# Fewer plain fp32 steps in block 0, zero matmuls in the prologue, new planner durations and other staging tiles in a pooled-attention and two-MLP kernel

## The chip, the cores and the metric

The kernel runs on one NeuronCore of one Trainium2 chip. The metric is the time of one execution in microseconds of the device (us), the median of several. Engine names are those of the profile: PE (matrix engine), DVE (vector engine), ACT (scalar engine), POOL, SP (here a queue that issues DMAs).

## What is computed

The reference pools keys and values over groups of 8 rows, does softmax attention for 8 batches of 8 heads, and passes the 4608 rows of 512 through two MLPs:

```python
k_p = k.reshape(B, H, Sp, pool, D).mean(axis=3)        # pool = 8, S = 576, D = 64
v_p = v.reshape(B, H, Sp, pool, D).mean(axis=3)
attn = softmax(scale * q @ k_p.T) ; x = attn @ v_p      # rows of all heads: 4608 x 512
h = x @ w_in                                            # 512 x 2048
g = where(h >= 1, h, where(h <= -1, 0, (h + 1)**2 / 4))
x = g @ w_out                                           # 2048 x 512
out = (sigmoid(x @ w_gate) * (x @ w_val)) @ w_out2      # 512 x 1536, twice, and 1536 x 512
```

The weights come in as float64 and are rounded on the chip.

## The kernel before, in words

**Blocks and steps.** The 4608 rows are nine blocks of 512. The first MLP runs blocks 0 to 6 one after the other (the rest goes through a form with seven products in place of eight, later in the program). A block has 16 steps, one for each 128 columns of `w_in`. A step m makes `hps` = 128 columns of x @ w_in (function `columns`), the activation g from it (L741 and L743 on ACT, L746 on DVE), and adds g times 128 rows of `w_out` to four accumulators (the out GEMM, L765 to L775).

**Three products or one.** A matmul of fp32 precision is made of three in a faster type (`three`, L609 to L611): each operand is split in a high part (a cast on ACT, L534) and a low part (a subtraction on DVE, L543). In the out GEMM of block 0 the first `PLAIN` = 12 steps skip this: they multiply the unsplit fp32 tiles (L772), so that neither g nor the `w_out` tile (`wj`) has to be split.

**Weights.** During block 0 all 16 tiles of `w_in` (`win`) and of `w_out` (`wout_f`) are loaded as float64 bit patterns and converted (function `weight`): two passes on ACT (L580, L582), four on DVE (L585, L587, L590, L594), and for `win` the split (L534, L543).

**Prologue.** Ahead of block 0 stand four units, one for each pair of heads: `pooled` sums the keys on DVE (L339) and turns them on PE (L360), sums the values either on PE (`add_values`, L375, eight matmuls with the identity) or, for the pairs in `DVE_VALUES` = (2, 3), on DVE (L339), and `unit` turns q (L407), makes scores (L436), softmax (L445 to L455, ACT L448), turns the weights (L470), multiplies by the values (L508) and splits the result into an x tile (L515, L522). Attention for the later blocks runs beside the first MLP in the same way (its transposes go to DVE, L424 and L481).

**Who sets the order.** Nothing is reordered on the chip. A planner written out in the kernel (class `Plan`) takes every operation with an engine, a duration in us, a due time (`key`), its reads and its writes, plays the program through with these durations, and puts on each engine the operation of the earliest due time among those ready. Its model of DMA has a rate (`RATE0`) until a time (`RAMP`). So a changed duration moves instructions on all engines, anywhere in the program.

**Row copies.** `out_rows` (L618) copies the four accumulators of a finished block to a staging tile and stores them: the first two rows to a tile `st` of its own, the others to a tile of the `raw` ring (2 tiles), which the weight loads use too.

Of the kernel before, what the change touches and what calls it, by code (L numbers as in the profile page):

```python
# [8 lines left out]
F32 = mybir.dt.float32  # L9
# [9 lines left out]
P = 128  # L19
# [8 lines left out]
RATE0, RAMP = 240e3, 30.0  # L28
# [179 lines left out]
def pooled_attention_two_mlps(  # L208
# [31 lines left out]
    DVE_VALUES = (2, 3)  # L240
    PLAIN = 12
# [44 lines left out]
    AC = {n: ac for n in ("kp", "q", "qT", "mx", "sm", "aq", "aT", "st")}  # L286
# [32 lines left out]
    def pooled(b, p, T):  # L319
# [65 lines left out]
    def unit(j, p, T):  # L385
# [10 lines left out]
        if first:  # L396
# [12 lines left out]
            op(PE, 1.05, T, transposes, r=[qb, ident], w=[ptq])  # L409
# [29 lines left out]
        op(PE, 1.15 if first else 0.6, T + 3, scores, r=[qT] + [kts[b % 2, p] for _, _, b, _ in segs], w=scs)  # L439
        for h in range(2):  # L440
# [6 lines left out]
            for t in range(NT4):  # L447
                op(ACT, 0.3 if first else 0.52, T + 5, lambda t=t, h=h, view=view, mx=mx: nc.scalar.activation(  # L448
# [13 lines left out]
        if first:  # L462

            flat = Src(aT, lambda t: t.rearrange("c a h t j -> c (a h t j)"))
            for h in range(2):
# [5 lines left out]
                op(PE, 1.02, T + 9, transposes, r=[e, ident], w=[pt])  # L471
# [39 lines left out]
        op(PE, 1.05 if first else 0.86 + 0.25 * (len(segs) > 1 and j % 2), T + 18 - AHEAD_PX * first, values,  # L511
# [35 lines left out]
    def reload(d, t, key, behind):  # L547
# [4 lines left out]
        op(ACT, 0.62, key - 2, lambda: nc.scalar.copy(out=t.t[:, 0], in_=vals()), r=[t], w=[t])  # L552
        op(DVE, 0.69, key - 1, lambda: nc.vector.tensor_tensor(
            out=t.t[:, 1], in0=vals(), in1=t.t[:, 0].bitcast(F32), op=ALU.subtract), r=[t], w=[t])

    def weight(w, m, cols, r, key, t=None, keep=None, spill=None):
# [37 lines left out]
        op(DVE, 0.7, key - 4, lambda: nc.vector.tensor_tensor(  # L594
# [18 lines left out]
    def columns(key, o, w, xs):  # L613
        last = []
        for c in range(KD):
            def mm(c=c):
                wv = view_cols(w)
                three(o.t, wv[:, 0, c], wv[:, 1, c], xs[c].t[:, 0], xs[c].t[:, 1], c == 0, c == KD - 1)  # L618
            last = [op(PE, 0.65, key + 0.1 * c, mm, r=[w, xs[c]], w=[o], behind=last)]

    def out_rows(key, dst, accs, d=(), early=False):
        for i in range(2):
            st = buf_a("st", 1, [P, 2, TB]) if early and i == 0 else Buf(raw_p, "raw", 2, [P, 2, TB], fifo=None if early else True)
            for n, a in enumerate(accs[2 * i:2 * i + 2]):
# [766 lines left out]
```

## Time and profile before

| | before |
|---|---|
| runs | 1691.58, 1692.19, 1692.28 us: median 1692.19 us |
| profiled execution | 1693.15 us, of which the span from first to last instruction is 1691.4 us |
| PE busy | 1667.2 us of the span (99%), 8484 instructions |
| DVE busy | 1168.6 us (69%) |
| ACT busy | 967.8 us (57%) |
| DMA | 396 MB, 234 GB/s on average |
| mean granted clock of PE | 0.996 of full speed |

Busy shares are averages over a program with several stages. In the 40 slices of the page (42 us each) DVE stands at 8 to 9 tenths in block 0 and at 4 to 8 later. "Granted clock" is the share of 2.4 GHz that PE gets; it has two levels here, 1.2 and 2.4 GHz. In the timeline a row gives the start, the time from the first start to the last end, the engine and line, the operation with its tiles, and the number of instructions; PE's matmuls overlap, so what one costs in a stream is the distance of starts. An unsplit fp32 matmul shows as two instructions.

### The profile page before, as it was taken

To read this page: it belongs to the slowest core of one execution; us is meant where nothing else is said; L and a number is where in the kernel's file an instruction comes from. 1 tells how busy PE (TensorE), PEld (TensorE's weight loads), DVE (VectorE), ACT (ScalarE), POOL (GpSimd) and SP (SyncE) were. 2 spreads that over 40 slices of the span, in tenths; PEclk is the share of its full clock that TensorE was granted. 3 is DMA by queue.
4 is the path that set the end of the run, shared out by engine and by line. 5 is a ranking of instruction groups with operands and counts; after the bars stand their busy time and mean duration, and the time that the engine had idled before them with its cause. 6 is when DMAs were issued, how large, how long until landed. Compare 5 with 4: busy or idle time off the path is not lost.

```text
span 1691.4 us, 26119 instructions
## 1 busy us (share of the span) xinstructions
PE 1667.2 (99%) x8484; PEld 1323.8 (78%) x8484; DVE 1168.6 (69%) x2166; ACT 967.8 (57%) x2140; POOL 238.3 (14%) x338
## 2 busy tenths in 40 slices
PE   7999999999999999999999999999999999999998
PEld 5657777777777777788888888878888888888886
DVE  7988767878787878846778856574448445744476
ACT  6767556676676668643466735454435454544344
POOL 1224323333433222100000002100000000000000
PEclk8999999999999999999999999999999999999999
DMA  8889867777877656547887879997889788977774
GB/s 218 246 250 244 203 138 203 230 217 195 233 201 191 175 162 211 175 159 303 326 275 239 292 237 370 360 343 215 234 257 304 211 238 274 280 194 205 206 219 135
DMA packets 308647, 396.07 MB, mean 234 GB/s; under 512 B 133664, under 2 KB 173856, under 8 KB 306976
## 3 DMA queue, kind: packets, MB, share of 16 engines
q1 hardware_dynamic: 270848, 285.97, 57.1%
q0 software_dynamic: 37664, 108.44, 20.6%
q8 instruction: 68, 1.11, 0.3%
q14 instruction: 67, 0.55, 0.1%
HBM read 272.11 MB, written 112.72 MB: 228 GB/s over the span
## 4 chain that ended last, share of the span: by engine, by line
PE 89%; DMA 5%; DVE 3%; SPq 1%; ACT 1%; issue 1%; POOL 0%; DVEq 0%; POOLq 0%; ACTq 0%
PE acc L609 12%; PE h L609 12%; PE acc L611 12%; PE acc L610 12%; PE h L610 11%; PE h L611 11%; PE a L609 5%; PE a L611 5%; PE a L610 5%; PE a L508 2%; DMA kv<-in_k_dram 2%; PE a L436 1%; PE acc L772 1%; DMA raw<-in_moe_w_out_dram 1%; SPq L487 1%
## 5 line engine op out<-in xcount | busy, mean ns | idle before, releaser
L834 DVE TENSOR_TENSOR g<-win,g 128x512 fp32r<-128x512 f32 x168 | 114.8, 689 | 113.1 <-ACT g L833 111.7
L609 PE MATMUL h<-x,win 128*128 128x512 f32 x448 | 183.4, 409 | 2.1 <-DVE t L746 2.1
L611 PE MATMUL h<-x,win 128*128 128x512 f32 x448 | 175.1, 391 | 1.3 <-DVE win L543 1.3
L610 PE MATMUL h<-x,win 128*128 128x512 f32 x448 | 175.3, 391 | 0.4 <-DVE x L522 0.4
L833 ACT CAST g<-win 128x512 fp32r<-128x512 f32 x168 | 104.3, 624 | 111.8 <-PE acc L611 90.5
L609 PE MATMUL acc<-g,wj 128*128 128x512 f32 x400 | 161.3, 403 | 0.0
L610 PE MATMUL acc<-g,wj 128*128 128x512 f32 x400 | 156.5, 391 | 0.0
L611 PE MATMUL acc<-g,wj 128*128 128x512 f32 x400 | 156.2, 391 | 0.0
L609 PE MATMUL acc<-g,wo 128*128 128x512 f32 x360 | 140.1, 389 | 0.7 <-ACT g L833 0.7
L611 PE MATMUL acc<-g,wo 128*128 128x512 f32 x360 | 140.1, 389 | 0.0
L610 PE MATMUL acc<-g,wo 128*128 128x512 f32 x360 | 140.1, 389 | 0.0
L609 PE MATMUL h<-x,ws 128*128 128x512 f32 x336 | 131.3, 391 | 0.4 <-ACT h L1335 0.4
L610 PE MATMUL h<-x,ws 128*128 128x512 f32 x336 | 131.0, 390 | 0.2 <-DVE x L829 0.2
L611 PE MATMUL h<-x,ws 128*128 128x512 f32 x336 | 130.8, 389 | 0.0
L741 ACT ACTIVATE t<-h,half 128x512 f32<-128x512 f32 x112 | 77.2, 689 | 89.0 <-PE h L611 88.0
L609 PEld LDWEIGHTS h<-x,win 128*128 128x128 f32 x448 | 84.1, 188 | 28.4 <-issue 6.0
L611 PEld LDWEIGHTS h<-x,win 128*128 128x128 f32 x448 | 84.1, 188 | 20.7 <-DVE win L543 2.6
L610 PEld LDWEIGHTS h<-x,win 128*128 128x128 f32 x448 | 84.2, 188 | 19.2 <-issue 2.4
L609 PEld LDWEIGHTS acc<-g,wj 128*128 128x128 f32 x400 | 75.1, 188 | 24.3 <-issue 7.4
L611 PEld LDWEIGHTS acc<-g,wj 128*128 128x128 f32 x400 | 75.1, 188 | 16.8 <-DVE wj L543 0.3
L534 ACT CAST wj<-wout_f 128x512 fp32r<-128x512 f32 x100 | 61.8, 620 | 43.4 <-PE acc L611 37.1
L610 PEld LDWEIGHTS acc<-g,wj 128*128 128x128 f32 x400 | 75.1, 188 | 14.6 <-DVE f L590 0.2
(308 smaller groups left out, 4062.0 us busy)
## 6 DMA issues: line engine op xcount, KB each, us to landing
ws<-seven SPq DMA_DIRECT2D x412, 256.0 KB
wo<-seven_o SPq DMA_DIRECT2D x144, 256.0 KB
seven<-f POOLq DMA_DIRECT2D x64, 256.0 KB, 3.8
seven<-wa POOLq DMA_DIRECT2D x8, 1792.0 KB, 7.7
seven_o<-wo POOLq DMA_DIRECT2D x42, 256.0 KB, 5.8
w<-f POOLq DMA_DIRECT2D x36, 256.0 KB, 4.2
wo<-seven SPq DMA_DIRECT2D x36, 256.0 KB
win<-in_moe_w_in_dram SPq DMA_DIRECT2D x16, 512.0 KB
```

The source lines that it names most:

```text
L436: nc.tensor.matmul(out=scs[h].t[r0 % P:r0 % P + D, r0 // P * C:r0 // P * C + C], lhsT=qT.t[D * h:D * h + D, r0:r0 + D], rhs=kts[b % 2, p]. ...
L487: op(SP, 0.65, T + 10, lambda a=a, bl=bl, n=n: nc.sync.dma_start(out=aT.t[32 * bl:32 * bl + n, a].rearrange("c h t j -> c (h t j)"), in_=a ...
L508: nc.tensor.matmul(out=px.t[D * h:D * h + D, lo:hi], lhsT=vps[b % 2, p].t[:, h], rhs=rhs, start=True, stop=True)
L534: ACT: (0.52, lambda: nc.scalar.copy(out=dst.t[:, 0], in_=src())),
L609: nc.tensor.matmul(out=o, lhsT=wh, rhs=xh, start=start, stop=False, skip_group_check=more)
L610: nc.tensor.matmul(out=o, lhsT=wh, rhs=xl, start=False, stop=False, skip_group_check=more)
L611: nc.tensor.matmul(out=o, lhsT=wl, rhs=xh, start=False, stop=stop, skip_group_check=more)
L741: op(ACT, 0.69, Tg, lambda t=t, hps=hps: nc.scalar.activation(out=t.t, in_=hps.t, func=AF.Relu, bias=half.t, scale=0.5), r=[hps, half], w=[t])
L772: nc.tensor.matmul(out=accs[c].t, lhsT=wj.t[:, c * P:(c + 1) * P], rhs=g.t, start=m == 0, stop=m == M1 - 1)
L833: op2(ACT, cost, key, lambda: nc.scalar.copy(out=out_hi(), in_=val()), r=[src, b], w=[b])
L834: op2(DVE, cost, key + 0.5, lambda: nc.vector.tensor_tensor(out=out_lo(), in0=val(), in1=out_hi().bitcast(F32), op=ALU.subtract), r=[src, ...
```

## The change

- `PLAIN` goes from 12 to 5: steps 5 to 11 of block 0's out GEMM take three products on split operands.
- `DVE_VALUES` becomes empty: the values of pairs 2 and 3 are summed on PE.
- `idle_columns` adds 29 matmuls of the identity with a tile of zeros (`e_sb`), into accumulator banks that nobody reads: five of 512 columns with a due time ahead of all else, 24 of 256 columns with a due time after the prologue's, which the planner puts where PE waits in its play.
- The planner's durations change (DVE's 0.69 to 0.61, ACT's 0.62 to 0.52, a product of three 0.65 to 0.68, and so on), and its DMA rate and ramp; no operation is made other by that, but the order of all later work is drawn up anew.
- `out_rows` of blocks 0 to 4 stages its rows in two free tiles of the `x` ring (8 tiles), that of block 5 in the `raw` ring; the tile `st` goes. The reloads of x for blocks 4 to 6 are put behind the row copies of the block two ahead.

```diff
-RATE0, RAMP = 240e3, 30.0
+RATE0, RAMP = 212e3, 14.0
...
-    DVE_VALUES = (2, 3)
-    PLAIN = 12
+    DVE_VALUES = ()
+    PLAIN = 5
...
-        op(DVE, 0.7, key - 4, lambda: nc.vector.tensor_tensor(
+        op(DVE, 0.6, key - 4, lambda: nc.vector.tensor_tensor(
...
     def out_rows(key, dst, accs, d=(), early=False):
+        rows = []
         for i in range(2):
-            st = buf_a("st", 1, [P, 2, TB]) if early and i == 0 else Buf(raw_p, "raw", 2, [P, 2, TB], fifo=None if early else True)
+            st = Buf(x_p, "x", 2 * KD, [P, 2, TB], fifo=None) if early > 0 else Buf(raw_p, "raw", 2, [P, 2, TB], fifo=None if early else True)
...
     zeros = memsets()
-    xs_of = {}
+
+    def idle_columns(n, key):
+        b = bank("acc")
+        op(PE, n / 1200, key, lambda: nc.tensor.matmul(
+            out=b.t[:, 0:n], lhsT=ident.t, rhs=e_sb.t.rearrange("p t h c -> p (t h c)")[:, 0:n], start=True, stop=True),
+            r=[ident, e_sb], w=[b])
+    for _ in range(5):
+        idle_columns(TB, -5)
+    for _ in range(24):
+        idle_columns(256, 25)
+    xs_of, rows_of = {}, {}
...
-                op(SP, 0.475, T - 16, lambda x=x, d=d: nc.sync.dma_start(out=x.t[:, 1].bitcast(F32), in_=d.t), r=[d], w=[x], nbytes=P * TB * 4)
+                op(SP, 0.475, T - 16, lambda x=x, d=d: nc.sync.dma_start(out=x.t[:, 1].bitcast(F32), in_=d.t), r=[d], w=[x], behind=rows_of[j - 2], nbytes=P * TB * 4)
...
-                last_y[c] = [op(PE, 0.9 if plain else 0.65, due1(s + 2) + 2.6 + 0.1 * c, mm, r=[wj, g], w=[accs[c]], behind=last_y[c])]
+                last_y[c] = [op(PE, 1.03 if plain else 0.68, due1(s + 2) + 2.6 + 0.1 * c, mm, r=[wj, g], w=[accs[c]], behind=last_y[c])]
...
-        out_rows(due1(s + 2) - 10, y_d[j].t, accs, [y_d[j]], j < NB1 - 1)
+        rows_of[j] = out_rows(due1(s + 2) - 10, y_d[j].t, accs, [y_d[j]], 1 if j + 2 < NB1 else -1 if j < NB1 - 1 else 0)
```

The lines of the changed kernel are some 12 higher from `out_rows` on: a zero matmul is L639, the plain out GEMM L784, the activation on DVE L758. What the order looks like at three places follows.

PE at the very start, before (L407 turns q, L360 the keys, L436 makes scores; `a` and `h` are accumulator banks, `kt` the turned keys):

```order
L407 MATMUL acc<-ident,q 128x128 x4
L360 MATMUL acc<-ident,kp 128x72
L407 MATMUL acc<-ident,q 128x128 x4
L436 MATMUL a<-kt_151,qT 64x72 x16
L360 MATMUL acc<-ident,kp 128x72
```

The same place in the changed kernel:

```order
L639 MATMUL acc<-e_sb,ident 128x512 x5
L407 MATMUL acc<-ident,q 128x128 x4
L360 MATMUL acc<-ident,kp 128x72
L639 MATMUL acc<-e_sb,ident 128x256 x3
L436 MATMUL a<-kt_151,qT 64x72 x16
L407 MATMUL acc<-ident,q 128x128 x4
L360 MATMUL acc<-ident,kp 128x72
L639 MATMUL acc<-e_sb,ident 128x256 x3
```

All 29 zero matmuls stand ahead of the first product of block 0, between matmuls of the units.

PE just ahead of block 0, before (L470 turns softmax weights, L375 sums values, L508 multiplies by values, `vp`):

```order
L470 MATMUL acc<-ident,g 72x128 x16
L375 MATMUL acc<-x,ident 72x128 x8
L508 MATMUL acc<-aT,vp_156 64x512 x2
L508 MATMUL acc<-aT,vp_154 64x512 x2
L470 MATMUL acc<-ident,g 72x128 x8
L609 MATMUL h<-x,win 128x512
```

And in the changed kernel:

```order
L470 MATMUL acc<-ident,g 72x128 x8
L375 MATMUL acc<-x,ident 72x128 x16
L508 MATMUL acc<-aT,vp_154 64x512 x2
L508 MATMUL acc<-aT,vp_156 64x512 x2
L470 MATMUL acc<-ident,g 72x128 x8
L375 MATMUL acc<-x,ident 72x128 x8
L639 MATMUL acc<-e_sb,ident 128x256 x2
L609 MATMUL h<-x,win 128x512
```

The values' sums of pairs 1 and 2 now stand together, and the last pair's stands behind the last transposes, two zero matmuls ahead of block 0.

DVE in the changed kernel, from the first split `win` tile on (L380 copies the last pair's summed values, which PE's last L375 makes; L594 is the row "ISA"):

```order
L543 TENSOR_TENSOR win<-f,win 128x512
L522 SCALAR_TENSOR_TENSOR x<-acc,x 128x512
L594 ISA wout_f_135<-raw,f 128x1024
L590 SCALAR_TENSOR_TENSOR f<-win,f 128x512
L380 COPY vp_158<-acc 72x128
L594 ISA f<-win,f 128x1024
```

and, some 70 rows on, around the activation of step 6:

```order
L758 SCALAR_TENSOR_TENSOR t<-t,h 128x512
L543 TENSOR_TENSOR win<-f,win 128x512
L594 ISA wout_f_141<-raw,f 128x1024
L543 TENSOR_TENSOR g<-t,g 128x512
L585 TENSOR_SCALAR f<-f 128x512
L543 TENSOR_TENSOR wj<-wout_f_140,wj 128x512
L587 TENSOR_SCALAR f<-f 128x512
L543 TENSOR_TENSOR wj<-wout_f_141,wj 128x512
```

Before, the values of this pair were summed on DVE itself (L339), ahead of the first place, and at the second no split of `g` or `wj` stood there. From the first split `win` tile to the sixteenth DVE has 199 instructions before and 215 in the changed kernel: seven splits of `g` and seven of `wj` more, a copy of keys and two of values more, one L587 fewer.

## Rows read from the trace of the kernel before

**Rows 1.** The page, part 1: busy time, share of the span, instructions of each engine.
```profile
span 1691.4 us, 26119 instructions
PE 1667.2 (99%) x8484; PEld 1323.8 (78%) x8484; DVE 1168.6 (69%) x2166; ACT 967.8 (57%) x2140; POOL 238.3 (14%) x338
```

**Rows 2.** What PE waited for: us in total, times, longest.
```profile
PE acc L407 <- DMA q<-in_q_dram: 7.3, 2, 6.0
...
PE h L609 <- DVE t L746: 2.1, 2, 1.8
PE h L611 <- DVE win L543: 1.3, 2, 1.1
```

**Rows 3.** Timeline of PE in the prologue: start, us, operation, instructions.
```profile
6.04 1.09 PE L407 MATMUL acc<-ident,q 128*128 128x128 f32 x4 [6.04 <-DMA q<-in_q_dram]
...
9.49 1.24 PE L436 MATMUL a<-kt,qT 64*64 64x72 f32 x32
...
11.75 0.73 PE L436 MATMUL h<-kt,qT 64*64 64x72 f32 x32
...
12.81 0.63 PE L407 MATMUL acc<-ident,wj 128*128 128x128 f32 x4
...
25.53 3.46 PE L470 MATMUL acc<-ident,g 128*72 128x128 f32 x16
28.83 1.91 PE L375 MATMUL acc<-x,ident 72*72 72x128 f32 x16
30.67 1.94 PE L508 MATMUL acc<-aT,vp 72*64 72x512 f32 x8
32.54 1.07 PE L470 MATMUL acc<-ident,g 128*72 128x128 f32 x8
33.36 0.48 PE L609 MATMUL h<-x,win 128*128 128x512 f32 x1
```

**Rows 4.** Stretches of the prologue: length, busy of five engines, granted clock, DMA share, GB/s.
```profile
24.00:27.00 3.00, 3.00 (x11) 1.29 (x8) 2.03 (x6) 2.03 (x10) 0.67 (x1) 0.50 0.46 74
27.00:30.00 3.00, 3.00 (x22) 2.75 (x21) 3.00 (x10) 3.00 (x14) 0.65 (x1) 0.72 0.87 209
30.00:33.00 3.00, 3.00 (x19) 1.45 (x18) 3.00 (x8) 2.46 (x6) 0.00 (x0) 1.00 1.09 297
```

**Rows 5.** The chain of work, 92.69 us: four unsplit matmuls of the out GEMM.
```profile
92.69 3.43 PE acc L772 x8
```

**Rows 6.** Timeline of PE: step 1's first product; step 2's second; its end.
```profile
39.43 0.40 PE L609 MATMUL h<-x,win 128*128 128x512 f32 x1
...
46.69 0.39 PE L610 MATMUL h<-x,win 128*128 128x512 f32 x1
...
49.23 1.04 PE L375 MATMUL a<-kv,ident 72*72 72x128 f32 x8
```

**Rows 7.** Stretches of block 0, columns as in rows 4 (PE, PEld, DVE, ACT, POOL).
```profile
27.00:42.00 15.00, 14.55 (x87) 9.43 (x85) 14.97 (x33) 13.17 (x33) 3.99 (x5) 0.94 0.99 254
42.00:58.00 16.00, 16.00 (x131) 10.06 (x129) 14.93 (x33) 11.99 (x35) 4.78 (x5) 1.00 0.91 263
34.00:143.50 109.50, 106.77 (x610) 65.83 (x609) 99.25 (x201) 79.73 (x202) 30.58 (x35) 1.00 0.88 247
```

**Rows 8.** Timeline of DVE: zero tile; first split `win` tile and next; the sixteenth.
```profile
1.00 0.70 DVE L316 MEMSET e_sb<- 128x768 f32 x1
33.41 0.68 DVE L543 TENSOR_TENSOR win<-f,win 128x512 fp32r<-128x512 f32 x1
34.00 0.68 DVE L522 SCALAR_TENSOR_TENSOR x<-acc,x 128x512 fp32r<-128x512 f32 x1
142.79 0.67 DVE L543 TENSOR_TENSOR win<-f,win 128x512 fp32r<-128x512 f32 x1
```

**Rows 9.** What DVE waited for most in 34 to 143.5 us: total, times, longest.
```profile
DVE win L543 <- ACT win L534: 4.7, 3, 2.4
```

**Rows 10.** PE and the others from the end of block 0 to the tail, columns as in rows 4.
```profile
154.00:1684.00 1530.00, 1523.18 (x7593) 1229.86 (x7592) 1037.03 (x1893) 860.47 (x1842) 201.84 (x292) 1.00 0.77 235
```

More of the change, by code (lines that the diff above doesn't have):

```diff
@@ L447, in unit @@
             for t in range(NT4):
-                op(ACT, 0.3 if first else 0.52, T + 5, lambda t=t, h=h, view=view, mx=mx: nc.scalar.activation(
+                op(ACT, 0.3, T + 5, lambda t=t, h=h, view=view, mx=mx: nc.scalar.activation(
                     out=e.t[:, t, h, 0:C], in_=view()[:, t], func=AF.Exp,
@@ L551, in reload @@
            r=[d], w=[t], behind=behind, nbytes=P * DM * 4)
-        op(ACT, 0.62, key - 2, lambda: nc.scalar.copy(out=t.t[:, 0], in_=vals()), r=[t], w=[t])
-        op(DVE, 0.69, key - 1, lambda: nc.vector.tensor_tensor(
+        op(ACT, 0.52, key - 2, lambda: nc.scalar.copy(out=t.t[:, 0], in_=vals()), r=[t], w=[t])
+        op(DVE, 0.61, key - 1, lambda: nc.vector.tensor_tensor(
             out=t.t[:, 1], in0=vals(), in1=t.t[:, 0].bitcast(F32), op=ALU.subtract), r=[t], w=[t])
@@ L914, in out_part @@
         g = buf_g()
-        op2(ACT, 0.62, key - 5, lambda: nc.scalar.copy(out=g.t[:, 0], in_=gs.t[:, f]), r=[gs], w=[g])
-        op2(DVE, 0.69, key - 4, lambda: nc.vector.tensor_tensor(
+        op2(ACT, 0.52, key - 5, lambda: nc.scalar.copy(out=g.t[:, 0], in_=gs.t[:, f]), r=[gs], w=[g])
+        op2(DVE, 0.61, key - 4, lambda: nc.vector.tensor_tensor(
             out=g.t[:, 1], in0=gs.t[:, f], in1=g.t[:, 0].bitcast(F32), op=ALU.subtract), r=[gs, g], w=[g])
@@ L922, in mm @@
                       w.t[:, 0], w.t[:, 1], m == 0, m == M2 - 1)
-            last[c] = [op(PE, 0.65, key + 0.1 * c, mm, r=[w, g], w=[accs[c]], behind=last[c])]
+            last[c] = [op(PE, 0.68, key + 0.1 * c, mm, r=[w, g], w=[accs[c]], behind=last[c])]
     lasts = [[] for _ in range(4)]
@@ L1009, in comb @@
         def comb(key, h, n, x, y, alu, other=None):
-            op2(DVE, 0.69, key, lambda: nc.vector.tensor_tensor(out=h.t[:, n], in0=x(), in1=y(), op=alu),
+            op2(DVE, 0.61, key, lambda: nc.vector.tensor_tensor(out=h.t[:, n], in0=x(), in1=y(), op=alu),
                 r=[h] + ([other] if other else []), w=[h])
@@ L1033, in mm @@
                               start and i == 0, i == MP - 1, not start)
-                chain[:] = [op2(PE, 1.3, key, mm, r=[w, g] + ([] if start or i else o), w=o, behind=chain)]
+                chain[:] = [op2(PE, 1.36, key, mm, r=[w, g] + ([] if start or i else o), w=o, behind=chain)]
                 if (n, i) == MARK:
@@ L1174, in minus @@
         def minus(o, x, y, key, name):
-            op2(DVE, 0.69, key, lambda: nc.vector.tensor_tensor(out=o[0](), in0=x(), in1=y(), op=ALU.subtract),
+            op2(DVE, 0.61, key, lambda: nc.vector.tensor_tensor(out=o[0](), in0=x(), in1=y(), op=ALU.subtract),
                 r=[a, b], w=[o[1]])
@@ L1284, in mm @@
                                   start and k == 0, k == 1, not start)
-                    op(PE, 1.3, T + H * pos, mm, r=[w] + xx + ([] if start else [o]), w=[o])
+                    op(PE, 1.36, T + H * pos, mm, r=[w] + xx + ([] if start else [o]), w=[o])
                 def add(key, o, b, u):
-                    op2(DVE, 0.69, key, lambda: nc.vector.tensor_tensor(out=o.t, in0=b.t, in1=u.t, op=ALU.add),
+                    op2(DVE, 0.61, key, lambda: nc.vector.tensor_tensor(out=o.t, in0=b.t, in1=u.t, op=ALU.add),
                         r=[b, u], w=[o])
@@ L1328, in keep @@
                     if kind == "in":
-                        op2((ACT, DVE), (0.6, 0.69), key, (lambda: nc.scalar.copy(out=u.t, in_=b.t),
+                        op2((ACT, DVE), (0.485, 0.61), key, (lambda: nc.scalar.copy(out=u.t, in_=b.t),
                                                            lambda: nc.vector.tensor_copy(out=u.t, in_=b.t)), r=[b], w=[u])
                     else:
-                        op2(ACT, 0.6, key, lambda: nc.scalar.copy(out=u.t, in_=b.t), r=[b], w=[u])
+                        op2(ACT, 0.485, key, lambda: nc.scalar.copy(out=u.t, in_=b.t), r=[b], w=[u])
                 def to_bank(key, src, dst):
```

51 lines of the change are left out of this document (26 added, 25 removed).

## The prediction

> **What bounds the kernel now.** I read the page's first part, then PE's waits, then the timelines of PE and DVE from the start to the end of block 0, then the stretches. PE is busy 1667.2 of 1691.4 us [rows 1]: the 24.2 us without it are the whole that better overlap could give, and 7.3 of them are the wait for the first loads of q [rows 2]. So time can come only from less work on PE, from its clock, or from waits. From 154 us to the tail PE is idle 1530.00 - 1523.18 = 6.8 us [rows 10]. What the change does lies almost all ahead of that, in two stages.
>
> In the **prologue** PE begins at 6.04 us [rows 3] and block 0's first product starts at 33.36 us. Its clock matters there: sixteen score matmuls take 1.24 us at 9.49 and 0.73 at 11.75 us [rows 3], so the array came to full speed some 5.7 us after it began; later it fell back, and the granted clock reads 0.50 at 24 to 27 us and 1.00 from 30 us on [rows 4].
>
> In **block 0** two engines are nearly full. From 34 to 143.5 us PE is busy 106.77 of 109.50 us and DVE 99.25 [rows 7]. DVE splits its first `win` tile at 33.41 us and its sixteenth at 142.79 [rows 8]: 109.4 us with some 10.2 idle. PE waits for DVE's splits of `win` already (1.3 us in all [rows 2]); with 9% less to spare on DVE the roles would change.
>
> **The change, part by part.**
>
> *Steps 5 to 11 on PE.* Four unsplit matmuls take 3.43 us [rows 5]. Eleven split ones fill the 2.54 us from 46.69 to 49.23 us [rows 6], 0.23 each, so the twelve that replace them take 2.77. The gain is 7 x 0.66 = 4.6 us of PE.
>
> *The same steps on DVE and ACT.* Seven splits of g and seven of `wj` go ahead of the sixteenth `win` split. One costs DVE 0.59 (starts at 33.41 and 34.00 [rows 8]): 14 x 0.59 = 8.3 us. The three small copies less one L587 are about 0.5, an estimate by their sizes beside that row. ACT gets 14 casts; it is busy 79.73 of 109.50 us [rows 7], so I cost them at nothing, covered by some 30 us that ACT has free; without that cover 14 x 0.6 = 8 us.
>
> *The prologue on PE.* The 29 zero matmuls are unsplit fp32, like L772: 3.43 / 4 = 0.86 us for 512 columns, 0.43 for 256 [rows 5]. The planner counts n/1200, half of that (0.43 and 0.21). So they do not fit the gaps they were laid in, and each pushes what stands behind it: 5 x 0.86 + 24 x 0.43 = 14.6 us. The real work at full clock is, ahead of the first product, four times L407 (0.5, from the 0.63 at 12.81), L360 (0.1, an estimate by its 72 columns beside L407's 512) and L436 (0.66, from 0.73), four L470 of 0.82 (32.54 to 33.36), four L375 of 1.84 (28.83 to 30.67; two of them came over from DVE), and three L508 of 0.94 (30.67 to 32.54, two of them) [rows 3]: 2.0 + 0.4 + 2.6 + 3.3 + 7.4 + 2.8 = 18.5 us. The zero tile is ready at 1.70 us [rows 8], so PE starts at 1.8 in place of 6.04. While the clock comes up it runs at half: over the same 5.7 us as before [rows 3] that costs 2.9 us (between 1.5 and 8.6, all five at half speed). Sum: 1.8 + 14.6 + 18.5 + 2.9 = 37.8 us for the first product, 4.4 later than 33.36. Loads don't hold it up, since each unit's q and k land before their new turn. Step 0 then runs without the slow start it had (33.36 to 39.43 us, 6.1 us [rows 3, 6], against 12 x 0.23 + 0.94 = 3.7): step 1 starts at 41.5 against 39.43, 2.1 later.
>
> *What now ends block 0.* By PE alone, the sixteenth `win` tile would be wanted 2.1 - 4.6 - 1.3 (its old waits) = 3.8 us earlier than before, near 139 us. By DVE it can't be there. DVE's copy L380 waits for PE's last L375, which ends two zero matmuls (0.86) ahead of 37.8, at 36.9; DVE passes at 37.3. Four instructions since the first `win` split (2.4 us) are done by then. The work from first to sixteenth `win` split was 99.2 us (109.4 less 10.2) and is 99.2 + 8.3 + 0.5 = 108.0, so 105.6 are left, and the sixteenth split starts at 142.9 us plus DVE's idle time: 142.79 before. So **the gain of PE is eaten by DVE**: 0.1 us later plus what idle time DVE keeps. When DVE was the bound (27 to 42 us) it kept 0.03 of 15 us, when PE was (42 to 58) 1.07 of 16 [rows 7]: over 105.6 us that is 0.2 to 7.1, and the most it can keep is what it had, 10.2. It will be the bound, so I stay near the low end, but ACT's late casts (4.7 us [rows 9]) come in part from loads that don't get faster: 1.2. Block 0 thus ends 1.3 us later. After the sixteenth split no weight of `win` is left to make, PE has the same work as before and DVE has room again.
>
> *The rest.* Row copies in x tiles: the same copies and the same 18 stores, nothing, hidden beside PE; if a reload of x waited behind them, one copy of 0.59. Their gain, a free `raw` ring, and the new order of everything later are worth between -6.8 us (all idle of [rows 10] gone) and about as much lost; I take 0, since no view says which waits the new order leaves.
>
> **Sum:** 1693.15 (profiled execution) + 1.3 = 1694.5 us; that execution is 0.96 above the median of the runs, so against 1692.19 I say 1693.5 us. A measurement of this kernel can tell about 0.2%, 3.4 us.
>
> **Rivals.**
>
> *DVE keeps its idle time (slower).* Place: DVE between `win` splits in block 0, in order behind ACT's casts, which wait for loads and for PE. It decides from 3.3 us of idle left on; at 42 to 58 us DVE left 6.7% [rows 7]. With 6 us left: 1692.2 + 6.1 = 1698.3 us. For it speaks that every queue is in order, against it that a late DVE gives loads and ACT time. 24%.
>
> *Later waits go too (faster).* DVE runs like at 27 to 42 us (0.2 us left) and the new order removes two thirds of the 6.8 us [rows 10]: 1692.2 + 0.3 - 4.6 = 1687.9 us. For it: the largest of these waits, 1.8 us [rows 2], is one of PE for DVE's activation. 19%.
>
> *The zero matmuls cost what the planner says, 14.6 / 2 = 7.3 us less, or fit idle time after all (faster).* The first product starts near 32 us and DVE's copy by up to 5 us earlier: 1692.2 + 1.3 - 5.0 = 1688.5 us. L772 speaks against it [rows 5]. 8%.
>
> *Zeros don't hold the clock (much slower: the change doesn't do what it says).* The prologue then runs at half: by up to 33.1 us longer, at least by the 2.9 again. With half of it, 1692.2 + 1.3 + 16.6 = 1710.1 us. No row shows a matmul on zeros. 4%. The Trainium skill ("TensorE: Matmul & The Clock Gate", Part 1) ties the clock to how busy the array is; by that this rival falls away, and no run here shows it yet.
>
> *Transposes don't hold the clock.* With all 8 groups of transposes at half, 2.0 + 3.3 = 5.3 us more ahead of L380: 1692.2 + 1.3 + 5.3 = 1698.8 us. Against it, the clock rose from 0.50 to 1.00 while the array had done nothing but L470 since 25.53 us [rows 3, 4]. 2%. That is a rule of the Trainium skill (the same page, Part 4: transposes are not counted as busy in the same way); this trace speaks against it.
>
> **How the numbers follow.** The forecast, DVE as the new bound, has 43%. Slower by over 0.2%: 24 + 4 + 2 = 30%. Faster: 19 + 8 = 27%. The range of 8 in 10 reaches from 1686.5 (a little below the faster cases) to 1700.5 (above the 1698.3 of the idle-time rival and the 1698.8 of the transposes), and leaves out the cold prologue and the far ends of the later waits. The likeliest case's own range is 1690.5 to 1696.
>
> **What would show it.** Right: zero matmuls of 0.86 and 0.43 us apart; first product at 37 to 39 us; granted clock 1.00 from about 8 us on; DVE over 97% busy from 37 to 143 us, PE idle there by some 5 us more than before, with DVE's `win` and g splits as releasers; the sixteenth `win` split near 144 us. Wrong: a first product ahead of 34 us, or DVE idle over 3 us in block 0, or PE's idle time after 154 us far from 6.8.

## The result and the profile after

| | before | after |
|---|---|---|
| runs beside each other | 1692.19 us (1689.79 to 1694.17, 5 runs) | 1717.39 us (1712.11 to 1721.44, 5 runs) |
| ratio, 95% interval | | 1.0145 [1.012, 1.017] |
| profiled execution / span | 1693.15 / 1691.4 us | 1713.31 / 1711.5 us |

The change makes the kernel 1.5% slower; the forecast said no change that can be measured, with a range up to 1700.5 us. The profiled execution is one of the quicker ones of its kernel. Its span is 20.1 us longer than that of before. The page of after, part 1 (as [rows 1]):

```profile
span 1711.5 us, 26379 instructions
PE 1681.2 (98%) x8602; PEld 1341.7 (78%) x8602; DVE 1169.5 (68%) x2169; ACT 982.8 (57%) x2161; POOL 236.9 (14%) x338
```

PE is 14.0 us longer busy and 6.1 us longer idle. To see where, I divided both spans at the same three instructions: the first product of block 0, of block 1 (step 16) and of step 108, in the last block of the plain form. Stretches of before, then of after (columns as in [rows 4]: length, busy of PE, PEld, DVE, ACT and POOL, granted clock, DMA share, GB/s):

```profile
0.00:33.36 33.36, 23.68 (x224) 17.83 (x225) 22.76 (x56) 20.69 (x86) 2.02 (x7) 0.80 0.84 210
33.36:145.91 112.55, 109.80 (x624) 68.09 (x622) 102.30 (x208) 81.17 (x204) 30.58 (x35) 1.00 0.89 248
145.91:713.64 567.73, 565.13 (x3384) 441.25 (x3383) 449.28 (x942) 381.74 (x1010) 176.08 (x241) 1.00 0.72 195
713.64:1691.40 977.76, 968.55 (x4257) 796.64 (x4255) 594.22 (x963) 484.21 (x842) 29.59 (x56) 1.00 0.80 256
```

```profile
0.00:37.25 37.25, 35.40 (x314) 26.43 (x315) 25.23 (x61) 21.92 (x87) 2.96 (x9) 1.00 0.83 204
37.25:152.65 115.40, 107.81 (x651) 74.03 (x650) 107.01 (x218) 85.87 (x212) 32.43 (x37) 0.99 0.88 249
152.65:729.27 576.62, 568.68 (x3384) 444.64 (x3383) 448.98 (x937) 390.10 (x1018) 172.99 (x239) 0.99 0.70 193
729.27:1711.50 982.23, 969.28 (x4257) 796.63 (x4255) 588.25 (x955) 484.95 (x846) 28.49 (x54) 1.00 0.79 253
```

The losses are 3.9 (prologue), 2.9 (block 0), 8.9 (blocks 1 to 6) and 4.5 us (the rest). In the last two stretches PE does the same number of matmuls (3384, 4257), so nothing there is work that the change added: idle time grows by 5.3 and 3.7 us, and the busy time of blocks 1 to 6 by 3.6 at a clock of 0.99. **Two thirds of the loss lie where the diff adds no work at all.** How the loss falls to the stages is that of one execution: a_dur2old and a_mid below have after's order up to block 1 and start it at +11.7 and +16.1 us, where after's profile has +6.7.

**The prologue came as forecast.** Timeline of PE of after (as [rows 3]): the first four and the next six instructions of the zero matmuls, two for each, then the way into block 0:

```profile
1.85 3.69 PE L639 MATMUL acc<-e_sb,ident 128*128 128x512 f32 x4 [1.85 <-DVE e_sb L316]
5.37 2.74 PE L639 MATMUL acc<-e_sb,ident 128*128 128x512 f32 x6
7.94 0.60 PE L407 MATMUL acc<-ident,q 128*128 128x128 f32 x4
...
37.25 0.58 PE L609 MATMUL h<-x,win 128*128 128x512 f32 x1
```

The first four take 3.52 us, 0.88 each, the other six 2.57, 0.43 each: PE starts at the lower level, 1.2 GHz, and comes to full speed while it does nothing but matmuls on zeros. The granted clock reads 1.00 from 0 on, but that says nothing of the first 5 us: in before it reads 1.00 at 8 to 10 us too, where the scores run at half speed [rows 3]. From 5.34 us to block 0 it is 1.00 (in before 0.50 at 24 to 27 us [rows 4]). The first product stands at 37.25 us.

**Block 0.** Its sixteenth `win` split is at 149.50 us, 6.7 later than before ([rows 8]). Timeline of DVE at that split, DVE's stretch up to it, and what DVE waited for there:

```profile
149.50 0.69 DVE L543 TENSOR_TENSOR win<-f,win 128x512 fp32r<-128x512 f32 x1
```
```profile
37.30:149.50 112.20, 105.35 (x641) 72.00 (x639) 103.81 (x210) 84.29 (x206) 31.59 (x36) 0.98 0.87 248
```
```profile
DVE g L543 <- ACT g L534: 2.8, 3, 1.5
DVE t L758 <- ACT t L755: 1.7, 4, 0.9
DVE sm L452 <- ACT e_sb L448: 1.6, 1, 1.6
```

DVE is busy 103.81 us and idle 8.4. The largest stall of PE there, in its timeline:

```profile
86.92 0.39 PE L611 MATMUL h<-x,win 128*128 128x512 f32 x1
89.42 1.30 PE L508 MATMUL a<-aT,vp 72*64 72x64 f32 x12 [2.11 <-ACT e_sb L448]
...
90.65 0.80 PE L609 MATMUL h<-x,win 128*128 128x512 f32 x1
91.24 0.63 PE L610 MATMUL h<-x,win 128*128 128x512 f32 x1
91.67 0.63 PE L611 MATMUL h<-x,win 128*128 128x512 f32 x1
...
94.17 0.40 PE L611 MATMUL acc<-g,wj 128*128 128x512 f32 x1
```

After the wait of 2.11 us the products follow each other at 0.43 us in place of 0.23 until 93.80: PE runs at the lower of its two levels (granted clock 0.51 from 90.60 to 94.10 us). From the product at 90.65 to that at 94.17 us eight of them take 3.5 us in place of 8 x 0.23 = 1.8, so the stall costs 3.8 us, not 2.1. The chain of waits leads from this e_sb by way of DVE back to one load of `win` (start, us, what):

```profile
67.26 10.31 DMA win<-in_moe_w_in_dram
```

**Blocks 1 to 6.** What PE waited for between 150 and 715 us in after (total, times, longest); before, [rows 2] has 2.1 us for `t` as the largest:

```profile
PE a L508 <- DMA aT<-aq: 3.7, 3, 2.5
PE a L436 <- DVE kt L367: 2.8, 2, 2.0
```

The largest, in the chain of waits (twelve issues of `aT` on SP from 431.63 us on, some 0.6 us each, then the landing of the last) and in the stretches around it and around the one of `kt` at 588.38 us:

```profile
438.55 6.04 DMA aT<-aq
444.93 1.13 PE a L508 x14
```
```profile
440.00:450.00 10.00, 7.45 (x48) 5.28 (x51) 4.83 (x10) 3.71 (x8) 4.87 (x6) 0.83 0.84 267
590.00:600.00 10.00, 10.00 (x47) 7.57 (x46) 7.73 (x17) 7.84 (x26) 2.15 (x4) 0.88 0.73 229
```

Both waits are followed by the lower clock again. The first ends on the landing of `aT` itself. The second does not end on a transfer of its own: PE turned these keys at 585.13 us (L360), and DVE comes to their copy (L367) 3 us later, behind other work, the last of it a conversion that waited for ACT:

```profile
587.76 0.43 DVE L585 TENSOR_SCALAR f<-f 128x512 f32<-128x512 f32 x1 [0.44 <-ACT f L580]
588.10 0.23 DVE L367 TENSOR_SCALAR kt<-a 128x72 f32<-128x72 f32 x1
```

### The profile page after: what moved, and what is told of

Same layout as the page of the kernel before. It is cut to its first block, busy times and chain, and to the rows that moved or that the text cites. A ratio compares the mean times of both kernels' runs of the same rounds, so it can differ in the third digit from the quotient of the medians.

```text
span 1711.5 us, 26379 instructions
## 1 busy us (share of the span) xinstructions
PE 1681.2 (98%) x8602; PEld 1341.7 (78%) x8602; DVE 1169.5 (68%) x2169; ACT 982.8 (57%) x2161; POOL 236.9 (14%) x338
## 4 chain that ended last, share of the span: by engine, by line
PE 76%; DMA 10%; DVE 5%; issue 3%; SPq 3%; ACT 3%; POOL 0%; DVEq 0%; POOLq 0%; ACTq 0%
PE acc L609 10%; PE h L609 10%; PE acc L610 10%; PE acc L611 10%; PE h L610 9%; PE h L611 9%; PE a L609 4%; PE a L611 4%; PE a L610 4%; SPq L487 2%; DMA wa<-w 2%; PE a L508 1%; DMA aT<-aq 1%; PE acc L639 1%; PE a L436 1%
## 5 line engine op out<-in xcount | busy, mean ns | idle before, releaser
L609 PE MATMUL acc<-g,wj 128*128 128x512 f32 x428 | 172.1, 402 | 0.0
L611 PE MATMUL acc<-g,wj 128*128 128x512 f32 x428 | 167.8, 392 | 2.1 <-DVE wj L543 2.1
L610 PE MATMUL acc<-g,wj 128*128 128x512 f32 x428 | 168.1, 393 | 0.0
L758 DVE SCALAR_TENSOR_TENSOR t<-t,h 128x512 f32<-128x512 f32 x107 | 72.8, 680 | 41.4 <-ACT t L755 40.6
L609 PEld LDWEIGHTS acc<-g,wj 128*128 128x128 f32 x428 | 81.0, 189 | 22.9 <-issue 4.0
L611 PEld LDWEIGHTS acc<-g,wj 128*128 128x128 f32 x428 | 80.9, 189 | 20.3 <-DVE wj L543 2.8
L610 PEld LDWEIGHTS acc<-g,wj 128*128 128x128 f32 x428 | 81.1, 189 | 15.8
```

The costliest lines, as they stand in the source:

```text
L609: nc.tensor.matmul(out=o, lhsT=wh, rhs=xh, start=start, stop=False, skip_group_check=more)
L610: nc.tensor.matmul(out=o, lhsT=wh, rhs=xl, start=False, stop=False, skip_group_check=more)
L611: nc.tensor.matmul(out=o, lhsT=wl, rhs=xh, start=False, stop=stop, skip_group_check=more)
L758: op(DVE, 0.61, Tg + 2, lambda t=t, hps=hps, o=o: nc.vector.scalar_tensor_tensor(out=o.t, in0=t.t, scalar=1.0, in1=hps.t, op0=ALU.min, op1 ...
```

## The experiments

Offsets below are starts of the same product against the profiled execution of before, in us: "step 0", "step 1", "step 16" (block 1) and "step 108"; the last number is the end of the span. After: +3.9, +2.0, +6.7, +15.6, +20.1. Two parts of the change have no run of their own: the planner's DMA rate (`RATE0`, `RAMP`) and the values moved to PE (`DVE_VALUES`).

### One part of the change alone, on the kernel before

**b_plain5**: `PLAIN = 5`, nothing else.

> The kernel before with PLAIN = 5 alone. Theory DVE (the seven split steps overload DVE in block 0 and that is the main loss): PE loses 4.6 us of work, DVE gains 8.3 us against 10.2 us of idle time, the sixteenth win split comes 3 to 7 us later than 142.8 and the time is 3 to 8 us over the kernel before (1695 to 1700 us). Theory PLAN (the new durations and not the split steps make the loss): the planner, with its old durations, lays the splits out in time, and the time is within 3 us of the kernel before.

Measured 1705.8 us, 1.007 [1.005, 1.0089]; -0.9, -0.4, **+2.0**, +3.1, +8.0. The sixteenth split is at 144.80 us, 2.0 later than before. The time is above what either theory allows; the profiled execution (1701.2 us) is the quickest of the four.

**b_dur**: the new numbers of the planner alone (all lines of the diff that change only a duration; the DMA rate stays the old one).

> The kernel before with the planner's new durations alone; no operation is another. Theory PLAN: the order drawn up with them makes PE wait for attention (L436, L508) and loads; 8 to 20 us slower than before, with PE idle after 154 us up from 6.8 to 12 us or more. Theory DVE: an order of the same work, within 4 us of before. Theory ROWS (row copies in x tiles and the reloads behind them make the later waits): within 4 us of before as well.

Measured 1722.07 us (1713.9 to 1729.5), 1.0169 [1.0131, 1.0208]; +1.5, +5.6, +8.4, +20.9, +31.4. A table of numbers, with no operation made other (a few change between DVE and ACT), costs as much as the whole change: 28.7 us over the median of before, with 25.2 for the change, and the intervals overlap.

**b_rows**: the row copies in x tiles and the reloads behind them.

> The kernel before with the row copies in x tiles, and the reloads of x put behind them, alone. Theory ROWS: the waits of PE between 420 and 640 us appear here, 5 to 10 us slower. Theories DVE and PLAN: within 3 us of before, or a little faster since the raw ring is freer.

Measured 1702.59 us, 1.0061 [1.0041, 1.0082]; -1.2, -1.0, **-2.6**, +0.1, +8.9. Its loss lies between 780 and 860 us, in the second MLP. There PE's timeline and the stretches on both sides show:

```profile
782.25 0.50 PE L611 MATMUL a<-x,wb 128*128 128x512 f32 x1 [2.57 <-DVE wb L831]
```
```profile
770.00:780.00 10.00, 9.68 (x43) 7.70 (x41) 2.48 (x7) 3.60 (x6) 0.00 (x0) 1.00 0.93 320
780.00:790.00 10.00, 7.75 (x27) 6.20 (x28) 9.97 (x18) 4.84 (x7) 1.07 (x2) 0.83 0.44 184
```

DVE, busy 2.48 of the 10 us ahead, is busy 9.97 of the 10 us with the wait. What it waited for ahead of that is a load of `wb`, in its timeline:

```profile
777.84 0.42 DVE L881 TENSOR_TENSOR raw<-f,wb 128x256 f32<-128x256 f32 x1 [7.33 <-DMA wb<-w]
```

SP issues the two transfers of this `wb` at 766.07 and 768.09 us; in before they stand at 757.49 and 758.71. The clock falls after the wait.

**b_idle**: the 29 matmuls on zeros alone.

> The kernel before with the 29 zero matmuls alone. By the sum of the prediction: 14.6 us of zero matmuls on PE, with two L375 groups less than in the whole change (3.7 us), so the first product at 33 to 34.5 us in place of 33.4 and the time within 3 us of before. If zero matmuls are a cost of their own right (theory PROLOGUE): the first product at 36 us or later and 3 us slower. If their clock is worth more than their time: first product at 31 us or earlier, and 2 us faster.

Measured 1712.49 us, 1.0121 [1.0095, 1.0147]; +9.7, +6.5, +5.3, +11.0, +17.7. None of the three theories has the first product at 43.0 us: here the planner lays 19 of the zero matmuls in one row just ahead of it (34.90 to 43.02 us).

The four parts cost 12, 29, 9 and 19 us each alone (against the median of before in the same runs); their sum is far above the 25 us of the whole. What they cost is not a property of each edit. **b_nudge** asks whether any newly drawn order costs as much: before with `WAIT = 0.06` in place of 0.05.

> The kernel before with one number of the planner moved by a hair (how near in time two operations must be for the due time to choose, WAIT, 0.05 to 0.06 us). No operation, duration or tile is other, only the order of the program. Theory TUNED (the order before is one lucky or well tuned draw; any new draw puts waits of PE at new places): 1700 to 1712 us, with PE idle after 154 us at 12 us or more in place of 6.8. Theory PLAN (the new durations as such are wrong for the chip): within 4 us of before.

Measured 1694.55 us, 1.0019 [1.0006, 1.0032]; -0.5, -0.3, -1.6, -1.3, -0.6. PE's order differs from 82 us on. This one new order costs nothing like 1%.

### One part taken out of the change

**a_olddur**: after with the old durations.

> The changed kernel with the planner's old durations. Theory PLAN: most of the loss goes, 1694 to 1702 us. Theory TUNED: another draw, 1702 to 1720 us, with waits of PE at other places than in the changed kernel.

Measured 1725.05 us, 1.0185 [1.0168, 1.0202]; +23.4, +20.2, +18.2, +36.0, +36.8. The first product comes at 56.7 us: with the old numbers the planner lays zero matmuls and units in another order, so the run says nothing about block 0. Blocks 1 to 6 lose 17.8 us with the old numbers too; behind step 108 it adds 0.8 us, as little as b_nudge. PLAN, as "most of the loss goes", falls.

**a_noidle**: after without the zero matmuls.

> The changed kernel without the 29 zero matmuls. By the prediction's sum the prologue loses 14.6 us of PE work, has half clock as before, and the first product comes at 31 to 34 us in place of 37.25; theory PROLOGUE (that carries through to the end): 3 to 6 us faster than the changed kernel. Theory TUNED: block 0 starts earlier, but the end moves by anything from -12 to +8 us.

Measured 1725.58 us (1709.18 to 1730.89), 1.0178 [1.0127, 1.023]; +3.7, +6.6, +9.8, +33.3, +37.7, of the slowest of the four executions. The first product stands at 37.06 us, 0.2 earlier than with them, though matmuls that the forecast put at 14.6 us are gone, and one L508 of the units even stands behind it. Timeline of PE and stretches of a_noidle, ahead of its step 0 and from there to step 1, then the same step of after:

```profile
31.81 1.98 PE L508 MATMUL acc<-aT,vp 72*64 72x512 f32 x4 [2.95 <-DVE vp L380]
33.72 3.69 PE L375 MATMUL acc<-x,ident 72*72 72x128 f32 x16
37.06 0.78 PE L609 MATMUL h<-x,win 128*128 128x512 f32 x1
```
```profile
30.00:38.00 8.00, 6.19 (x22) 4.45 (x23) 5.74 (x13) 2.82 (x5) 0.73 (x1) 0.54 1.03 269
```
```profile
37.06:46.03 8.97, 8.97 (x67) 5.01 (x65) 5.32 (x11) 2.60 (x5) 2.70 (x3) 0.59 0.86 243
```
```profile
37.25:41.43 4.18, 4.18 (x19) 2.54 (x17) 3.96 (x8) 2.36 (x5) 2.38 (x3) 1.00 1.03 254
```

A wait of 2.95 us is followed by the lower clock, and eight L375 take 3.34 us in place of 1.84 ([rows 3] as the forecast reads them). Up to the first product the zero matmuls pay for themselves and no more. Behind it they gain: a_noidle keeps the lower clock until 44.3 us, and its step 1 starts 4.6 us after that of after, though not by the clock alone, since it has more work of the units there (67 matmul instructions against 19). Whether any of this reaches the end is not shown.

**a_plain12**: after with `PLAIN = 12`.

> After with twelve plain steps in block 0's out GEMM in place of five: by the forecast's own terms DVE loses 8.8 us of work in block 0 and PE gains 4.6 us. Theory DVE-BOUND (DVE's work sets the end of block 0, its idle time is much the same): the sixteenth win split comes at 140 to 144 instead of 149.5. Rival IDLE (waits set it, and less work on DVE becomes more idle time): the split at 147 or later, DVE busy under 97 us in the stretch. b_plain5 alone had +2.0 at step 16.

Measured 1727.27 us, 1.0205 [1.0184, 1.0226]; +4.0, +2.1, +11.5, +26.6, +30.4. The sixteenth split comes at 151.57 us. With five plain steps the one order of after gave 149.50, and 154.54 and 156.90 in a_dur2old and a_mid below: with twelve it lies among these. Stretch of a_plain12 up to after's own sixteenth split:

```profile
37.30:149.50 112.20, 105.69 (x562) 64.07 (x561) 95.84 (x193) 73.42 (x176) 31.80 (x37) 0.97 0.88 244
```

DVE has 8.0 us less to do than in after (95.84 against 103.81) and is idle 16.4 us. DVE-BOUND asked for 140 to 144 us: DVE's work is not what ends block 0.

**a_dur2old**: after with the old durations in the second MLP alone. All engines have after's order through the first MLP.

> After with the old durations in the second MLP alone; the order is after's row for row up to the end of the first MLP, so step 108 stays at +15.6 (within 1 us). Theory DUR2 (the 4.5 us that after loses behind 720 come from the new durations there): the rest takes what it took before, span 1706 to 1708, ratio 1.009 to 1.011. Rival DRAW: the second MLP loses 3 us or more again, span 1710 or later.

Measured 1712.89 us (1709.46 to 1721.86), 1.0109 [1.0092, 1.0126]. The profiled execution is the slowest of the five: +3.9, +2.0, **+11.7**, +24.9, +28.7. The same instructions in the same order reach step 16 here 5.0 us later than in after's profile, and step 108 9.3 us later. Timeline of DVE at the sixteenth split:

```profile
154.54 0.68 DVE L543 TENSOR_TENSOR win<-f,win 128x512 fp32r<-128x512 f32 x1
```

The ratio lies where DUR2 put it (1.009 to 1.011). Behind step 108 the profile adds 3.8 us (after 4.5), as the rival has it, and the runs' ranges overlap those of after. This run does not decide between the two.

### Is it that results come later than planned?

**a_slack3**: after, the planner lets every transfer land 3 us later:

```diff
-                free[eng], o.end = max(t, lanes[-8] + lat), lanes[-1]
+                free[eng], o.end = max(t, lanes[-8] + lat), lanes[-1] + 3.0
```

> The changed kernel with every DMA of the planner landing 3 us later (in the changed kernel the planner lets the aT copies land some 1.7 us after their issue, the trace shows 6.04). Theory LANDING (PE's later waits come from landings that the planner takes too early): the waits of L508 for aT and of L436 for kt go, 6 to 10 us faster than the changed kernel, 1705 to 1711 us. Theory TUNED: those waits go too, but others come, 1708 to 1725 us.

Measured 1715.74 us (1715.48 to 1716.13), 1.0137 [1.0122, 1.0152]; +7.4, +5.1, +14.8, +11.4, +22.8. From step 16 to 108 it *gains* 3.4 us on before, where after lost 8.9; the waits on `aT` and `kt` are gone. The prologue, block 0 and the second MLP lose more than after, so that in all it is no quicker, as TUNED has it.

**a_mid**: the same 3 us only for `150 < t < 715` of the planner's clock.

> After, but the planner takes every transfer to land 3 us later than its sum says while its clock stands between 150 and 715 us (blocks 1 to 6); up to there the order is after's row for row. After lost 8.9 us between step 16 (+6.7 against before) and step 108 (+15.6). Theory LANDING (the loss in blocks 1 to 6 is that PE meets aT and kt before their transfers have landed): the waits on aT and kt (6.5 us in blocks 1 to 6) are gone, step 16 at +6.7, step 108 at +4 to +8, span 1701 to 1705. Rival DRAW (any newly drawn order loses some us somewhere in these blocks, whatever the planner takes for a landing): step 108 at +12 to +18 with other waits in their place, span 1708 to 1715.

Measured 1708.67 us (1703.85 to 1711.86), 1.009 [1.0069, 1.0112]; +3.7, +1.8, +16.1, +12.4, +18.7. From step 16 to 108 again -3.7, and PE is not idle there at all:

```profile
162.06:726.01 563.95, 563.95 (x3384) 441.61 (x3383) 443.76 (x921) 386.30 (x1014) 170.41 (x234) 1.00 0.70 192
```

Step 16 came late for another reason: the cast that starts a conversion in ACT's timeline, first in a_mid, then in after:

```profile
151.71 0.66 ACT L580 ACTIVATE f<-raw 128x512 f32<-128x512 f32 x1 [6.23 <-DMA raw<-in_moe_w_out_dram]
```
```profile
144.27 0.67 ACT L580 ACTIVATE f<-raw 128x512 f32<-128x512 f32 x1 [0.67 <-DMA raw<-in_moe_w_out_dram]
```

DVE, ACT and SP have the same order up to there in both kernels. SP issues this 512 KB load at 137.39 us in after and at 140.69 in a_mid, behind eight stores of 256 KB (L772), and the cast that waits for it starts 6.9 and 11.0 us after the issue. DVE's sixteenth split, in order behind, goes from 149.50 to 156.90 us.

**a_lat**: DVE's and ACT's results planned 0.09 us after the engine is free. Timeline of DVE in after shows why one number cannot be both:

```profile
84.09 0.68 DVE L758 SCALAR_TENSOR_TENSOR t<-t,h 128x512 f32<-128x512 f32 x1
84.69 0.68 DVE L543 TENSOR_TENSOR win<-f,win 128x512 fp32r<-128x512 f32 x1
```

One takes 0.68 us, the next starts after 0.60. The old 0.69 is the first, the new 0.61 about the second.

```diff
                 free[eng] = o.end = self.array(t, cost, o.share) if eng == "pe" else t + cost
+                o.end += 0.09 * (eng in ("act", "dve"))
```

> After, but the planner lets the result of a DVE or ACT instruction be there 0.09 us after the engine is free again. In after's trace the starts of DVE's 512-column instructions follow each other at 0.60 us while one takes 0.685 (ACT: 0.57 at 0.68), and the new numbers of the table (0.61, 0.585, 0.53, 0.52) are the spacings, used for the engine and for the result alike. Theory SPACING (DVE's idle time in block 0 is that results are planned 0.07 to 0.10 us before they come, so that whoever is placed right behind waits): DVE's waits on ACT's g, t and e_sb in block 0 fall from 6.1 us to under 3, the sixteenth win split moves from 149.5 to 144 to 147, and the whole is 3 us or more under after. Rival DRAW: DVE keeps 7 us or more of idle time in 37 to 150, the sixteenth split stays at 148 or later.

Measured 1716.68 us, 1.0145 [1.0116, 1.0174]; +4.4, +3.2, **+2.5**, +14.6, +24.8. The sixteenth split stands at 145.26 us. DVE's longest wait for ACT up to it and the stretch (lines are one higher in this kernel):

```profile
DVE sm L453 <- ACT e_sb L449: 0.7, 1, 0.7
```
```profile
37.05:145.26 108.21, 104.51 (x648) 71.57 (x646) 103.48 (x210) 85.13 (x209) 31.24 (x35) 1.00 0.90 252
```

DVE is busy as long as in after and idle 4.7 us in place of 8.4; blocks 1 to 6 and the second MLP lose 12.1 and 10.2 us instead. In this execution the theory held in block 0. But a_lat_late and a_lat_late_d2 below have the same order up to step 16, and there the split stands at 151.24 and 151.75 us, later than in after's profile: what a_lat gained is within what the executions of one order differ by. Timeline of DVE in a_lat_late:

```profile
151.24 0.68 DVE L544 TENSOR_TENSOR win<-f,win 128x512 fp32r<-128x512 f32 x1
```

Three runs tried the theory further.

**a_lat_plain12**: a_lat with `PLAIN = 12`.

> a_lat with twelve plain steps in place of five. a_plain12 showed that with the spacings as the numbers DVE's missing 7 us of work became idle time (busy 96.6 of 113 us, split at 151.6). Theory SPACING (results planned too early make DVE's idle time; with 0.09 us more on them DVE's work sets the end of block 0 again): DVE's idle time up to the sixteenth win split stays at 6 us or less, the split comes at 138 to 143 against 145.26 in a_lat. Rival ARRIVALS (late transfers set it whatever DVE has to do): DVE idle 10 us or more, the split at 146 or later.

Measured 1729.72 us, 1.0241 [1.0217, 1.0264]; +4.0, +2.9, +11.6, +26.5, +31.7. The split is at 149.74 us; stretch:

```profile
37.30:149.50 112.20, 105.53 (x561) 63.19 (x560) 95.95 (x195) 73.38 (x177) 32.46 (x37) 0.97 0.88 243
```

DVE is idle 16.2 us again, and the split lies among those of five plain steps (145.26 to 151.75). SPACING falls as the general cause. For the rival speaks that between 37 and 158 us ACT waits 17.1 us for loads of weights (`f` for `raw` 7.0, `win` 5.2, `raw` 4.9), 9.7 in before; in after's profile, however, it is 4.7, so late loads alone do not explain the block 0 of after.

**b_dur_lat**: b_dur with the same 0.09 us.

> Before with the new durations alone (b_dur: +8.4 us at step 16, +20.9 at step 108, 1.0169 in all) and the results of DVE and ACT planned 0.09 us after the engine is free. Theory SPACING: step 16 at +4 or less, ratio under 1.012. Rival DRAW: step 16 at +6 or more, ratio 1.014 or more.

Measured 1726.15 us, 1.0214 [1.0191, 1.0237]; +4.6, +6.4, +14.8, +35.6, +39.2. Behind b_dur at each of these places; from step 108 on it loses less (3.7 us against 10.5). SPACING asked for +4 or less at step 16.

**a_lat_late**: a_lat with the 3 us on transfers for `165 < t < 715`.

> a_lat (+2.5 us at step 16, +14.6 at step 108) with every transfer taken to land 3 us later while the planner's clock stands between 165 and 715 us. If SPACING and LANDING are two causes that stand beside each other: step 16 at +2 to +7, blocks 1 to 6 add under 2 us (a_mid and a_slack3: minus 3.7 and minus 3.4 from step 16 to 108), step 108 at +6 or less, span 1700 to 1705. Rival DRAW (blocks 1 to 6 lose again by other waits): step 108 at +11 or more.

Measured 1705.87 us (1704.62 to 1708.14), 1.009 [1.0075, 1.0105]; +4.3, +3.2, +8.4, **+5.5**, +11.4. Blocks 1 to 6 gain 2.9 us; step 16 comes 5.9 us later than in a_lat, with the same order up to there. With a_mid, whose ratio is 1.009 too, it is the quickest of the variants that hold the whole change (after 1.0145).

### The second MLP

**b_rows_n8** and **b_rows_n6**: b_rows with `WAIT` at 0.08 or 0.06 from 715 us on.

> b_rows (row copies in x tiles alone: minus 2.6 us against before at step 16, +0.1 at step 108, +8.9 at the end, 1.0061) with the planner's constant WAIT at 0.08 in place of 0.05 once its clock is past 715 us: the first MLP's order stays, the second's is drawn again. Theory DRAW2 (the 4 to 9 us that all changed kernels lose in the second MLP hang on the order drawn there, not on what the edits do): the second MLP's loss moves by 4 us or more, either way. Rival LASTING (it comes from what the first MLP leaves behind: late stores, other transfers): +7 to +10 at the end again.

> As b_rows_n8 with 0.06 in place of 0.05 (the constant that cost before itself 1.8 us at most in b_nudge). DRAW2: the loss behind step 108 moves by 4 us or more from 8.8. LASTING: it stays at 7 to 10 us.

Measured 1702.78 us, 1.0065 [1.0049, 1.0081], and 1705.25 us, 1.0076 [1.0061, 1.0091]; behind step 108 they lose 5.8 and 9.2 us (b_rows 8.8). Neither moved by the 4 us that DRAW2 asked for, and the wait on `wb` near 782 us stays (2.53 and 2.75 us). But up to some 800 us the order of both is that of b_rows, so that wait had to stay, and the two runs say nothing about it.

**a_lat_late_d2**: a_lat_late with the old durations in the second MLP.

> a_lat_late (step 16 +8.4, step 108 +5.5, end +11.4) with the old durations in the second MLP. DUR2 (the new durations there cost it): step 108 at +3 to +8, the second MLP adds 2 us or less in place of 5.9, end 1696 to 1701. DRAW2: it adds 3 us or more by other waits.

Measured 1709.68 us (1706.49 to 1713.22), 1.0099 [1.0083, 1.0116]; +4.7, +3.6, +8.9, +9.5, +20.0. The second MLP adds 10.5 us in this profile, of the slowest of the four executions, more than with the new durations (5.9), and the median is far from the 1696 to 1701 us that DUR2 asked for. DUR2 falls. From step 16 to 108, where the order is that of a_lat_late, this execution stands at +0.6 (a_lat_late -2.9).

No version beats before. b_nudge is nearest, and b_rows runs 2.6 us ahead of before at step 16 before the second MLP takes it back.

## Why the forecast was wrong, point by point

- **Prologue: right.** 37.8 us for the first product, measured 37.25; step 1 at 41.5, measured 41.43; L380 at 36.9, measured 36.85. The slow start cost less than its term: ten instructions took 6.09 us where at full clock they take 4.3, so 1.8 us in place of 2.9. The rivals on the clock fall: PE came to full speed at 5.37 us on zero matmuls alone, and the granted clock stays at 1.00 up to block 0. On transposes the Trainium skill ("TensorE: Matmul & The Clock Gate", Part 4) says that they are not counted as busy in the same way; here they stand among zero matmuls, so this run adds little to [rows 3, 4], which speak against it.
- **DVE's work in block 0: right in size.** 105.6 us forecast, 103.81 measured. That b_plain5, the five plain steps without the rest, has the sixteenth split at 144.80 us, near the forecast's 142.9 + 1.2 = 144.1, is luck: there DVE begins its `win` splits at 33.03 us, is busy 105.45 us up to the sixteenth and idle 6.3.
- **"DVE keeps 1.2 us idle": failed.** It kept 8.4, and 13.7 and 16.0 where a_dur2old and a_mid ran the same order. The term was taken near the low end (0.2 to 7.1 to 10.2) because DVE "will be the bound". That reason is wrong, not only the size: with 8 us less work (a_plain12, a_lat_plain12) DVE ended block 0 among the executions of the same kernels with five plain steps, and was idle 16 us. In the forecast's words the rival "DVE keeps its idle time" is what happened. Of its place, DVE in order behind ACT is what DVE's waits show; ACT behind loads is shown for the stall of 2.11 us and for a_mid, not for all of the 8.4 us, since in after ACT waits less for loads of weights than in before (4.7 us against 9.7).
- **Block 0 as one number: failed.** One order reached step 16 at +6.7, +11.7 and +16.1 (after, a_dur2old, a_mid), another at +2.5, +8.4 and +8.9 (a_lat, a_lat_late, a_lat_late_d2). In a_mid one 512 KB load accounts for 7.4 of the 9.4 us, issued 3.3 us later and with 11.0 us in place of 6.9 from its issue to the cast; in a_dur2old that cast did not wait for its load, and what came late there is open. The forecast compared sums of work and had no term for this spread.
- **"The rest: I take 0": failed, and it is two thirds of the loss.** +8.9 in blocks 1 to 6, +4.5 behind, where the bound was 6.8 in all. For blocks 1 to 6 the cause is shown: the planner takes transfers to land earlier than they do. The four runs that plan them 3 us later have -3.4, -3.7, -2.9 and +0.6 us there (the last two in one order); after and its six variants without that (a_dur2old, a_lat, a_olddur, a_noidle and the two with twelve plain steps) lose 8.9 to 23.5. Which wait it becomes differs: `aT` for its own landing and `kt` behind DVE's other work in after, mainly `kt`, `e_sb` and loads of v in a_dur2old. The bound was too small on two counts: PE's idle time alone grew by 9.0 us behind block 0 (between 154 and 1684 us it is 15.2 in place of 6.8), and the two waits followed by half clock cost another 1.7 us each, which a price by their length leaves out.
- **What stays open.** Why block 0 and the second MLP lose in most variants. Results planned too early (a_lat) explained block 0 in one execution and failed in the next two of the same order, in a_lat_plain12 and in b_dur_lat. The new durations do not explain the second MLP: with the old ones a_olddur adds 0.8 us there, but a_lat_late_d2 10.5 and b_rows 8.9. In b_rows a load of `wb` that is issued some 9 us later than before makes its first wait; why it is issued later, and whether the order drawn there makes the rest, b_rows_n8 and b_rows_n6 don't settle. The planner's new DMA rate and the values moved to PE were not tried alone. That before has few such waits is because its numbers and its order fit each other; b_nudge shows that this fit bears a small push, the single parts that it does not bear much more. That fit, and why it bears the one and not the others, was only argued.

## What to carry to other kernels

Where a planner sets the order, a changed number is a change of the whole program: price the later stages by running the numbers alone (here +29 us for a table and nothing else), not by the work that the diff adds. The engine with the most work need not be the bound: before its slack is spent, see what its idle time ends on, and take the spread of landings as part of the range. Compare variants stage by stage only against how far the executions of one order lie apart (here 9.4 us at step 16). Price a wait of PE with the clock that it loses, which here nearly doubled it.

## What was not expected of the hardware

- Matmuls on zeros bring PE to full speed and hold it there: with nothing but them from 1.85 to 7.94 us, their instructions lie 0.88 us apart at first and 0.43 from 5.37 us on.
- Waits of PE of 2.11, 2.55, 2.01, 2.57 (b_rows) and 2.95 us (a_noidle) were followed by the lower level, for some 3 to 4 us in the first three. One of 2.06 us was not:

```profile
119.56 0.50 PE L611 MATMUL acc<-g,wj 128*128 128x512 f32 x1 [2.06 <-DVE wj L543]
```
```profile
118.00:128.00 10.00, 8.44 (x37) 6.89 (x38) 9.72 (x20) 7.55 (x15) 3.73 (x5) 1.00 0.67 180
```

- DVE's 512-column instructions take 0.68 us each and start 0.60 us apart, so the durations of a page add up to more than the engine's time.
- One order, different executions: after's runs spread over 9.3 us, before's over 4.4. That its waits for loads are the reason is not shown; a_slack3, which plans every transfer 3 us later, spreads over 0.7.
